# When two batches' loads begin in a fused sparse attention and feed-forward kernel

## The chip, the cores and the metric

The kernel runs on one core of a Trainium2 chip. The metric is the device time of one execution in microseconds (us). TensorE (PE) does the matmuls and PE transposes, VectorE (DVE) and ScalarE (ACT) the elementwise work, GpSimd (POOL) casts and copies and issues casting DMAs on its own queue, and SyncE (SP) issues the other DMAs, loads, stores and DMA transposes. All queues share 16 DMA engines.

## The reference

Eight batches, eight heads, 576 positions, head width 64. The first four heads attend to the last 32 positions, the other four to every 32nd position. The attention output, 4608 tokens by 512, goes through two matrices with a squared ReLU between them.

```python
scores = scale * np.matmul(q, k.transpose(0, 1, 3, 2))
mask_local = (rel >= 0) & (rel < stride)                  # heads 0-3
mask_strided = (rel >= 0) & (pos[None, :] % stride == pos[:, None] % stride)   # heads 4-7
attn = exp(masked scores - max); attn = attn / sum
x = np.matmul(attn, v).transpose(0, 2, 1, 3).reshape(B * S, H * D)
h = x @ w_in                 # 512 -> 2048
r = np.maximum(h, 0.0)
out = (r * r) @ w_out        # 2048 -> 512
```

All inputs and the output are float32; the kernel computes in bf16 with float32 accumulation.

## The kernel before

**Units.** Work on attention is cut into units of one batch and two heads: unit `u = 4 * b + p`. Of a batch's four units the first two are local, the other two strided. Batch 1 is units 4 to 7, batch 2 is units 8 to 11, and so on. A unit goes through `step_T` (PE transposes of q and k, line 271, read from the casts `q_l`, `k_l`; strided units from batch 2 on use DMA transposes instead), `step_S` (scores, line 315, then exp on ScalarE and the mask on VectorE), `step_D` (probabilities times V, line 419, and the division) and `step_E` (transposes back into `xt`, line 451).

**Feed-forward.** Tokens are cut into nine chunks of 512. `mm1` (line 487) is x times w_in, `mm2` (line 527) g times w_out. One `mm1` or `mm2` of four matmuls is a group, and the list `groups` is the backbone of the program. The attention steps of the next batches are threaded between the groups: `due[n]` says how many steps must have been emitted before group n. TensorE executes in exactly this order, so a step whose data is late stops everything behind it.

**Loads.** They hang on the same list: `plan` hooks `loads(b)` before a given group, and the queues then execute in the order written. Batch 2's hook is group 8, batch 3's is `g_end + 2`, group 33; the hook for batch 3's DMA transposes lies six groups behind it (`transpose_str`, line 161). A hook says only where a load stands in its queue's order. For batches 1 and 2 there is a data gate beside that: in `load_qk_local` GpSimd copies one element of another tile into the buffer that the first q load will overwrite (line 112), so that SP's load of q must wait for that copy, the copy for the transfer that fills the tile it reads, and everything behind either waits too. The gate of batch 1 reads the third quarter of w_in.

```python
if gate is not None and name == "q":
    nc.gpsimd.tensor_copy(t[0:1, 0, 0:1], gate)
```

**What stands behind the gate.** `loads(1)` issues on GpSimd, in this order: first quarter of w_out, q and k of unit 6, second quarter, local V of units 4 and 5, casts for unit 4, third quarter, q and k of unit 7, casts for unit 5, fourth quarter, then V of units 6 and 7 in two loads each (`load_v_str_cast`, line 227, into `vss[2]` and `vss[3]`), then two shifts. `loads(2)` and `loads(3)` put local q and k on SP as float32 (line 113), strided V on SP (line 201), cast strided q and k to DRAM by GpSimd's queue (line 153), load local V on GpSimd's queue (line 214), and then on GpSimd cast q and k (line 123, `q_st` to `q_l`, `k_st` to `k_l`), shift V (line 221) and cast strided V (line 208). The strided V tiles of a batch are `vss[0]` and `vss[1]` for even, `vss[2]` and `vss[3]` for odd batches. Buffers `q_st` and `k_st` are two deep, so a batch's q and k may be loaded once the batch before has been cast.

**Stores.** An output block is copied from PSUM to a tile `y` (four buffers) and stored by SP (line 532), in order with the loads.

Of the kernel before, what the change touches and what calls it, by code (L numbers as in the profile page):

```python
# [14 lines left out]
def kernel(  # L15
# [21 lines left out]
    NBS = 2 * NJ  # L37
# [28 lines left out]
    vss = [singles.tile([SP_, NBS, VP], BF16, name=f"vs{i}") for i in range(NV)]  # L66
# [4 lines left out]
    w_in_b = singles.tile([128, 4, d_ff], BF16)  # L71
    w_out_b = singles.tile([128, 16, d_model], BF16)
# [85 lines left out]
    def transpose_str(b):  # L158
        for name in "qk":
            o = strT.tile([128, NJ // 2, 4 * SP_], BF16, name=f"{name}T_s")  # L160
            nc.sync.dma_start_transpose(out=o, in_=big.pop((b, name)))
            for i in range(2):
                st.setdefault(4 * b + 2 + i, {})[name + "T"] = o[:, :, 2 * SP_ * i:2 * SP_ * (i + 1)]

    def transpose_local(u):
        s = st[u]
        for name in "qk":
            if name == "k":
                full = kTl[v_slot(u)]
                dst = full[:, 32:32 + S]  # L170
            else:
                full = dst = qkT.tile([128, S], BF16, name="qk"[u % 2] + "T")
            nc.sync.dma_start_transpose(out=dst.rearrange("c (t p) -> c t p", p=QL),
                                        in_=s[name].rearrange("p t h d -> p (t h d)"))
            s[name + "T"] = full
# [452 lines left out]

    pool2 = (nc.gpsimd.tensor_copy, nc.gpsimd.tensor_copy)

    gates = {1: w_in_b[0:1, 0, 1024:1025], 2: w_out_b[0:1, 8, 0:1]}

    def loads(b):
        u = 4 * b
        for i in range(2):
            load_qk_local(u + i, nc.sync, gate=gates.get(b) if i == 0 else None)
        if b == 1:
            load_w_out(0)
            load_qk_str(u + 2)
            load_w_out(1)  # L640
            for i in range(2):
                load_v_local_cast(u + i)
            cast_qk_local(u, pool2)
            load_w_out(2)
            load_qk_str(u + 3)
            cast_qk_local(u + 1, pool2)
            load_w_out(3)
            for i in range(2):
                load_v_str_cast(u + 2 + i)
            for i in range(2):  # L650
                shift_v_local(u + i)
            return
        load_v_str(u + 2, nc.sync)
        load_v_str(u + 3, nc.sync)
        cast_str_dram(b)
        for i in range(2):
            load_v_local_cast(u + i)
        for i in range(2):
            cast_qk_local(u + i, pool2)
        for i in range(2):  # L660
            shift_v_local(u + i)
        for i in range(2):
            cast_v_str(u + 2 + i)

    def loads_qk(b):
        for i in range(2):
            load_qk_local(4 * b + i, nc.sync)
        cast_str_dram(b)
        for i in range(2):
            cast_qk_local(4 * b + i, pool2)  # L670

    def loads_v(b):
        for i in range(2):
            load_v_local(4 * b + i, nc.sync)
        for i in range(2):
            load_v_str(4 * b + 2 + i, nc.sync)
        for i in range(2):
            cast_v_local(4 * b + i)
        for i in range(2):
            cast_v_str(4 * b + 2 + i)  # L680
# [89 lines left out]
    done_prev, g_prev = 0, 0  # L770
# [3 lines left out]
    def at(n, fn):  # L774
        hooks.setdefault(n, []).append(fn)

    def plan(b, n0, g0, g1):
        if b < LB:
            at(n0, lambda: loads(b))
            if b >= XB:  # L780
                at(n0 + 6, lambda: transpose_str(b))
            return
        g = g0 + (g1 - g0) * 45 // 100
        at(g, lambda: loads_qk(b))
        at(max(g + 8, g0 + (g1 - g0) * 8 // 10), lambda: transpose_str(b))
        at(n0, lambda: loads_v(b))
        for i in range(2):
            at(g + 14 + 4 * i, lambda u=4 * b + i: transpose_local(u))

    plan(2, 8, 0, 0)  # L790
    for b in range(1, B):
        g_end, s_end = ready.get(b, starts[b] - (14 if b >= XD else 2)), ends[4 * b + 3]
        if b == 1:
            g_prev = 12
        total = sum(weights[g_prev:g_end])
        for g in range(g_prev, g_end + 1):
            due[g] = done_prev + (s_end - done_prev) * sum(weights[g_prev:g]) // total
        if b + 2 < B:
            plan(b + 2, g_end + 2, g_prev, g_end)
        done_prev, g_prev = s_end, g_end  # L800
    done = 0
    for n, g in enumerate(groups):
# [40 lines left out]
```

## Time and profile before

| | before |
|---|---|
| five runs, us | 312.52, 314.27, 318.18, 324.10, 325.07 |
| median, us | 318.18 |
| profiled execution: its time, its span | 312.52, 310.6 us |
| mean granted TensorE clock | 0.995 |
| busy: TensorE, VectorE, ScalarE, GpSimd | 296.3, 166.6, 162.7, 88.2 us |
| DMA packets' time, SP's and GpSimd's queue | 50.1% and 26.2% of 16 engines' span |

The span runs from the first to the last instruction of one execution; its time includes what lies around that. The profiled execution is also the fastest of the five. The chain of work that ended last lists, in order of time, what each piece of the end's history waited for; the timeline lists instructions with the idle time before them in brackets and what ended it; a window gives each engine's busy time in a stretch, and the clock granted to TensorE there. A DMA's time to landing runs from its issue to the event that its data is there.

### The profile page before, as it was taken

How to read it: one execution, taken by the hardware profiler on the slowest of the kernel's cores; microseconds unless marked ns; L12 is line 12 of the kernel's file. 1: busy time of each engine (PE TensorE's matmuls, PEld its weight loads, DVE VectorE, ACT ScalarE, POOL GpSimd, SP SyncE). 2: the span in 40 equal slices, each digit the busy share in tenths (PEclk: the TensorE clock that was granted, in tenths of full speed). 3: DMA queues.
4: the chain of work that ended last, by engine and by line, in shares of the span. 5: the costliest groups of instructions: out<-in, count | busy, mean ns of one | idle time of the engine just before them, and what ended most of it. 6: DMA issues, size and time to landing. Idle time of an engine off the chain costs nothing.

```text
span 310.6 us, 6150 instructions
## 1 busy us (share of the span) xinstructions
PE 296.3 (95%) x2326; PEld 149.0 (48%) x2368; DVE 166.6 (54%) x411; ACT 162.7 (52%) x338; POOL 88.2 (28%) x117
## 2 busy tenths in 40 slices
PE   7889897999999999999999999999999999999995
PEld 3544454544555544454454454444444444444444
DVE  7675755479866966666468676654422222222200
ACT  3966654487555765555555555555343434344311
POOL 8528853654720712381065033000000000000000
PEclk9999999799999999999999999999999999999999
DMA  8999999999999999999999792224122000000121
GB/s 143 171 207 237 198 187 252 208 266 189 201 157 221 235 190 147 206 232 210 164 228 203 162 205 77 73 72 55 53 80 80 34 37 34 34 34 36 39 96 68
DMA packets 92252, 44.40 MB, mean 143 GB/s; under 512 B 76544, under 2 KB 85536, under 8 KB 92032
## 3 DMA queue, kind: packets, MB, share of 16 engines
q1 hardware_dynamic: 72528, 32.98, 50.1%
q0 software_dynamic: 19552, 10.98, 26.2%
q8 instruction: 18, 0.29, 0.4%
q10 hardware_dynamic: 144, 0.07, 0.1%
q14 instruction: 10, 0.08, 0.1%
HBM read 36.70 MB, written 13.57 MB: 162 GB/s over the span
## 4 chain that ended last, share of the span: by engine, by line
PE 80%; DMA 13%; POOL 4%; issue 1%; DVE 1%; ACT 0%; DVEq 0%; POOLq 0%; ACTq 0%
PE ph L487 36%; PE py L527 26%; PE ph L527 8%; DMA vs<-in_v_dram 5%; DMA w_in_b<-in_moe_w_in_dram 4%; PE pt L419 4%; DMA w_out_b<-in_moe_w_out_dram 4%; PE pt L315 3%; PE pt L451 1%; PE pt L271 1%; POOL kT_s L133 1%; POOL qT_s L133 1%; PE pt L512 1%; PE ph L512 1%; POOL vs L227 1%
## 5 line engine op out<-in xcount | busy, mean ns | idle before, releaser
L487 PE MATMUL ph<-xt,w_in_b 128*128 128x512 bf16 x559 | 142.2, 379 | 1.1 <-issue 0.3
L493 ACT ACTIVATE r<-ph 128x512 bf16<-128x512 f32 x143 | 85.3, 597 | 94.2 <-PE ph L487 91.3
L494 DVE TENSOR_TENSOR g_sb<-r 128x512 bf16<-128x512 bf16 x144 | 71.6, 502 | 101.9 <-ACT r L493 101.2
L527 PE MATMUL py<-w_out_b,g_sb 128*128 128x512 bf16 x378 | 99.6, 379 | 1.1 <-issue 0.3
L487 PEld LDWEIGHTS <-w_in_b 128*128 128x128 bf16 x576 | 52.4, 98 | 56.6 <-issue 0.5
L527 PEld LDWEIGHTS <-g_sb 128*128 128x128 bf16 x560 | 51.0, 98 | 53.8 <-issue 0.7
L320 ACT ACTIVATE e<-pt 128x288 bf16<-128x288 f32 (+1 forms) x128 | 46.3, 406 | 14.7 <-PE pt L315 14.7
L527 PE MATMUL ph<-w_out_b,g_sb 128*128 128x512 bf16 x155 | 39.3, 386 | 0.6 <-issue 0.3
L419 PEld LDWEIGHTS <-e 128*128 128x128 bf16 (+1 forms) x392 | 21.0, 98 | 17.3 <-issue 2.8
L434 DVE TENSOR_TENSOR x_s<-pt,rinv 72x384 bf16<-72x384 f32 (+1 forms) x42 | 21.4, 509 | 1.4
L192 POOL CAST vl<-vl_st 128x768 bf16<-128x768 f32 x8 | 6.6, 828 | 48.6 <-DMA vl_st<-in_v_dram 24.8
L326 DVE TENSOR_TENSOR e<-e,mask_str 72x576 bf16<-72x576 bf16 x32 | 17.1, 540 | 3.4 <-ACT e L320 3.2
L123 POOL CAST k_l<-k_st 96x768 bf16<-96x768 f32 x14 | 12.8, 913 | 17.0 <-DMA k_st<-in_k_dram 16.3
L531 ACT COPY y<-py 128x512 f32<-128x512 f32 x25 | 14.6, 585 | 5.5 <-PE py L527 5.1
L326 DVE TENSOR_TENSOR e<-e,mask_loc 128x576 bf16<-128x576 bf16 x32 | 15.6, 488 | 2.7 <-ACT e L320 2.7
L433 DVE RECIPROCAL rinv<-pt 96x6 f32<-96x6 f32 (+2 forms) x70 | 12.7, 182 | 7.5 <-PE pt L419 7.3
L123 POOL CAST q_l<-q_st 96x768 bf16<-96x768 f32 x14 | 12.5, 890 | 13.0 <-DMA q_st<-in_q_dram 11.1
L434 DVE TENSOR_TENSOR x_l<-pt,rinv 96x384 bf16<-96x384 f32 x28 | 15.5, 553 | 1.0
L419 PE MATMUL pt<-vs,e 72*128 72x65 bf16 x224 | 13.7, 196 | 2.3 <-DMA vs<-in_v_dram 2.2
L531 ACT COPY y<-ph 128x512 f32<-128x512 f32 x10 | 5.9, 587 | 16.0 <-PE ph L527 16.0
L208 POOL CAST vs<-v_st 72x1024 bf16<-72x1024 f32 x12 | 13.2, 1127 | 0.7 <-PE pt L451 0.4
L419 PE MATMUL pt<-vl,e 128*128 128x65 bf16 x168 | 9.8, 193 | 0.6 <-POOL vl L221 0.5
(91 smaller groups left out, 166.0 us busy)
## 6 DMA issues: line engine op xcount, KB each, us to landing
out_dram<-y SPq DMA_DIRECT2D x35, 256.0 KB, 2.9
v_st<-in_v_dram SPq DMA_DIRECT2D x12, 288.0 KB
q_st<-in_q_dram SPq DMA_DIRECT2D x16, 144.0 KB, 5.0
k_st<-in_k_dram SPq DMA_DIRECT2D x16, 144.0 KB, 7.0
vl_st<-in_v_dram SPq DMA_DIRECT2D x16, 144.0 KB, 3.0
w_in_b<-in_moe_w_in_dram POOLq DMA_DIRECT2D x4, 512.0 KB, 11.4
w_out_b<-in_moe_w_out_dram POOLq DMA_DIRECT2D x4, 512.0 KB, 10.4
q_st<-in_q_dram SPq DMA_DIRECT2D x7, 288.0 KB, 7.1
```

The source lines that it names most:

```text
L123: copy(t.rearrange("p j h d -> p h j d"), s[name + "f"].rearrange("p h (j d) -> p h j d", j=6))
L208: (copy or nc.gpsimd.tensor_copy)(t[:, :, 0:D], s["vf"].rearrange("p h (j d) -> p (h j) d", d=D))
L320: nc.scalar.activation(e[0:kn, lo:lo + S // 2], banks[row][half][0:kn, 0:S // 2], AF.Exp, scale=scale)
L326: nc.vector.tensor_tensor(x, x, m.to_broadcast([kn, n, w]), op=ALU.mult)
L419: nc.tensor.matmul(po[:, n - n0, :], e[0:kn, pos(n):pos(n) + 128], rhs[0:kn, src(n), 0:D + 1], start=True, stop=True)
L433: nc.vector.reciprocal(rinv[0:w, 0:m], po[0:w, 0:m, D:D + 1])
L434: nc.vector.tensor_tensor(x, po[0:w, 0:m, 0:D], rinv[0:w, 0:m].to_broadcast([w, m, D]), op=ALU.mult)
L487: nc.tensor.matmul(ph, w_in_b[:, kk, 128 * ff:128 * (ff + 1)], xt[kk][:, 512 * c:512 * (c + 1)], start=(kk == order[0]), stop=(kk == order ...
L493: nc.scalar.activation(r, ph, AF.Relu)
L494: later(1, lambda: nc.vector.tensor_tensor(g[:, ff, :], r, r, op=ALU.mult))
L527: nc.tensor.matmul(py, g[:, ff, 128 * j:128 * (j + 1)], w_out_b[:, ff, :], start=(ff == 0), stop=(ff == 15))
L531: nc.scalar.copy(y, py)
```

## The change

Two expressions. The gate of batch 2's loads reads an element of `vss[3]` that the last V load of batch 1 writes (its second half, `NBS - 1 = 15`), where it read the first element of the third quarter of w_out. And the hook of batch 3's loads is group 30 where it was 33, with its transposes at 36 where they were at 39; later batches keep their places.

```diff
-    gates = {1: w_in_b[0:1, 0, 1024:1025], 2: w_out_b[0:1, 8, 0:1]}
+    gates = {1: w_in_b[0:1, 0, 1024:1025], 2: vss[3][0:1, NBS - 1, 0:1]}
...
         if b + 2 < B:
-            plan(b + 2, g_end + 2, g_prev, g_end)
+            plan(b + 2, g_end + (2 if b > 1 else -1), g_prev, g_end)
```

In the emitted program TensorE's, VectorE's and ScalarE's instructions and their order are the same. On GpSimd the one copy reads another tile. On SP batch 3's six loads (four of q and k, two of V) stand ahead of the fourth output store instead of behind it.

## The prediction

> **What bounds the kernel now.** I read the page first: busy shares and the slices.
>
> ```profile
> PE 296.3 (95%) x2326; PEld 149.0 (48%) x2368; DVE 166.6 (54%) x411; ACT 162.7 (52%) x338; POOL 88.2 (28%) x117
> ...
> PE   7889897999999999999999999999999999999995
> ...
> PEclk9999999799999999999999999999999999999999
> DMA  8999999999999999999999792224122000000121
> ```
>
> TensorE is busy 95% of 310.6 us, so nothing later than the first 60 us has much to give. One slice (the eighth, 54 to 62 us) has a lower granted clock. Up to about 185 us the DMA engines are full: what a transfer gets, another loses. Next the chain of work that ended last, for the place where TensorE waits for a transfer; its longest single piece is (start, length, what):
>
> ```profile
> 38.68 15.29 DMA vs<-in_v_dram
> ```
>
> Then the timeline there, and the same microseconds as windows (PE busy, PEld, DVE, ACT, POOL, granted clock, DMA share, GB/s):
>
> ```profile
> 41.06 0.40 POOL L112 CAST q_st<-w_out_b 1x1 f32<-1x1 bf16 x1
> 41.49 0.31 SPq L113 DMA_DIRECT2D q_st<-in_q_dram  x1
> 50.51 0.82 POOL L123 CAST q_l<-q_st 96x768 bf16<-96x768 f32 x1 [3.14 <-DMA q_st<-in_q_dram]
> 54.01 0.31 PE L419 MATMUL pt<-vs,e 72*128 72x65 bf16 x5 [2.15 <-DMA vs<-in_v_dram]
> 57.53 0.69 PE L271 MATMUL pt<-ident,q_l 96*128 96x96 bf16 x6
> 59.46 0.42 PE L271 MATMUL pt<-ident,k_l 96*128 96x96 bf16 x6
> 63.03 0.42 PE L271 MATMUL pt<-ident,k_l 96*128 96x96 bf16 x6
> ```
>
> ```profile
> 55.00:56.00 1.00, 1.00 (x14) 0.79 (x12) 0.28 (x2) 0.26 (x1) 0.46 (x1) 0.64 0.80 169
> 56.00:57.00 1.00, 1.00 (x4) 0.30 (x2) 0.93 (x4) 0.00 (x0) 0.82 (x1) 0.50 1.61 153
> 57.00:58.00 1.00, 1.00 (x8) 0.62 (x7) 0.17 (x1) 0.00 (x0) 0.00 (x0) 0.50 2.34 149
> 58.00:59.00 1.00, 0.89 (x12) 0.74 (x12) 0.00 (x0) 0.69 (x2) 0.48 (x1) 0.65 0.72 31
> ```
>
> TensorE stands 2.15 us for unit 7's V (the last of batch 1), and then runs at half clock. Adding what is missing from 1.00 in the four windows, 0.36 + 0.50 + 0.50 + 0.35, gives 1.7 us. The stop so costs 3.8 us. The gate copy that today starts batch 2's loads ran at 41.06; batch 2's first cast (q of unit 8) waited for its data until 50.51, 9.0 us after issue, its k until 52.05. TensorE wanted them at 57.53 and 59.46: some 6 us of slack.
>
> **Part 1: the gate reads V instead of w_out.** No instruction is added; one 0.40 us copy on GpSimd waits for another transfer. The four V loads land, from the view of their tile and of single issues, 11.2, 10.9, 11.3 and 15.3 us after issue, that is at 46.6, 47.7, 49.2 and 54.0:
>
> ```profile
> L227 POOL DMA_DIRECT2D vs<-in_v_dram x4: 804/809/828, 35.4 to 38.7; - x4
> ...
> DMA to landing us min/median/max: 10.9/11.3/15.3
> ```
>
> The first three are 1.1 and 1.5 us apart, the last is 4.8 behind, just when SP's queue starts to move batch 2 (its first packets show between 45 and 46 us). Taking that traffic away, the last V lands early at 48.0 (most of the V packets, all under 512 B, had moved by 46; two us for the end), late at 54.0 (the tail is its own queue's). I take 49.5: near 38.68 + 10.9. TensorE wants V at 51.9, so the 2.15 us and the 1.7 us of slow clock go: -3.8 us, with 2.4 us of cover.
>
> The pause and the clock have a rule too. The Trainium skill (TensorE: Matmul & The Clock Gate, Part 1: The HAM clock gate) says that the clock halves after about 3.4 us idle; here 2.15 us were followed by 0.50 from 55 to 58.6 us. By the rule alone a pause this short need not cost clock, and the gain would be 2.15 us; the measured row decides.
>
> **What the later gate queues up.** On GpSimd behind the copy: two casting DMAs of q and k to DRAM, two loads of local V, four casts, two shifts, two V casts, and all of batch 3. On SP behind its wait for that copy: batch 2's q, k and strided V loads, two transposes, the output stores, batch 3's loads. All move from 41.5 to 49.9 us, 8.4 later, against a TensorE that comes 3.8 us sooner. Without the stop it would want q of unit 8 at 54.4, k at 55.7, unit 9's q at 56.8 and k at 59.2.
>
> How fast do they land in an emptier queue? Two other batches say:
>
> ```profile
> 22.93 0.31 SPq L113 DMA_DIRECT2D q_st<-in_q_dram  x1
> 27.65 0.85 POOL L123 CAST q_l<-q_st 96x768 bf16<-96x768 f32 x1
> 29.82 0.98 POOL L123 CAST k_l<-k_st 96x768 bf16<-96x768 f32 x1 [1.33 <-DMA k_st<-in_k_dram]
> ...
> 61.67 0.49 SPq L113 DMA_DIRECT2D q_st<-in_q_dram  x1
> 65.37 0.98 POOL L123 CAST q_l<-q_st 96x768 bf16<-96x768 f32 x1 [0.33 <-DMA q_st<-in_q_dram]
> 70.55 1.11 POOL L123 CAST k_l<-k_st 96x768 bf16<-96x768 f32 x1 [4.21 <-DMA k_st<-in_k_dram]
> ```
>
> Batch 1 had its first k 6.9 us after the first issue, batch 3 8.9; q came after at most 4.7 and 3.7. Batch 2 itself took 9.0 and 10.6, but behind the V loads. I take 4.2 for q and 7.9 for k, between the two emptier cases. Then q of unit 8 lands at 54.1, its cast (0.85) ends at 54.9: 0.5 us late. k lands at 57.8, cast until 58.7, wanted at 56.2: 2.5 late. Unit 9's q (about 9.5 after issue, then 0.85) is there at 60.2, wanted at 59.8: 0.4 late; its k (11.4 in batch 3) at 62.2, wanted 62.6: in time. So 3.4 us of the 3.8 come back, as the same kind of stop one transfer later. Bounds: nothing comes back but 0.5 (gate at 48.0, batch 1's pace: k cast by 56.2), or all and more (next part, third rival). Whether the new 2.5 us pause also costs clock, as the 2.15 did, would add up to 1.7; several short pauses with work between I cost at 0.
>
> The rule against waiting: the Trainium skill (DMA: Bandwidth & Descriptors, Anatomy of one DMA) puts about 2.0 us of fixed time on each DMA, which a load that starts only after another has landed pays in series. By its formula 288 KB would take 2.7 us (an estimate), q would be ready by 53.4 and its 0.5 us of lateness gone; no row here shows one so quick.
>
> Further behind: local V for unit 8 is issued at about 51 and lands 11.7 (batch 1) to 13.3 (batch 3) later, 62.7 to 64.3, then a 0.7 us shift; wanted at 67.2 less 0.4: covered by about 2 us, 0 if TensorE keeps the whole gain. The transposes for unit 10 were issued by 59.5 and used at 70.26; about 4 us later they are still covered.
>
> **Part 2: batch 3 three groups sooner.** Nothing is added; one 256 KB store of SP's goes behind six loads, and two transposes are queued sooner. On GpSimd batch 3's DMAs (62.25) already followed batch 2's last cast (60.28, 2.02 long) without a gap, so the sooner place brings nothing there; on SP at most one store's issue, 0.5 us. With batch 2's tail some 4 us later, batch 3 is later, not sooner; its tightest use is k of unit 12, cast until 71.7 and wanted at 78.98: 7.3 us of cover. The delayed store holds a y buffer not needed before 81.47. Cost 0; if that cover is gone, a stop of the size it is short.
>
> **Sum.** -3.8 + 3.4 = -0.4 us on the profiled 312.52 us (span 310.6): 312.1. That execution is the fastest of five (312.52 to 325.07); the median lies 5.7 above. Only this transfer-paced stage shows where a slower run can lose time: V has no reserve before, 2.4 us after. I let a third of the 5.7 remain, 1.9: 314.0. That third is a choice, between none and all (312 to 318).
>
> **The rivals.**
> - *Full gain* (0.25). Gate at 48.0, batch 1's pace: only 0.5 comes back, 309.2; with at most 1 us of the runs' offset, 310. For it: V's packets were nearly all through by 46. Against: DMA engines stand idle while the gate's landing is awaited (46 to 50 us moved 0.9 MB before).
> - *Batch 2 late* (0.22), the slower side. If the loads need as long after the gate as they do now (9.0, 10.6, about 13.1 and 14.4) with V at 50.3 and the copy done at 50.7: q of unit 8 cast by 60.6, wanted 54.4, 6.2 us; k 0.2 more; unit 9's q at 64.6, wanted 63.2, 1.4 more. -3.8 + 7.8 + 1.7 of clock = +5.7, 318.2; with the whole offset of 5.7, 324. It decides from k of unit 8 cast after 59.5 on: 55.7 + 3.8. For it: four casting loads share the engines. Against: V is no longer in front of them.
> - *V no sooner* (0.08). The change does not do what it says: V at 54.0, no gain, gate copy done at 54.4, q 2.0, k 1.8 and unit 9's q 0.4 late: +4.2, 316.7, with the offset 322.
> - *Forecast* (0.45): the stop moves from V to k. Own range 310 to 319.
>
> **How the numbers follow.** A difference of about 2% (311.8, 324.5) is what a measurement of this kernel can tell. Faster: 0.12 of the forecast and 0.23 of full gain, 0.35. Slower: 0.02 of the forecast, 0.20 of late batch 2, 0.05 of the late V, 0.27. Within: 0.38. Range: from the full gain with no offset, rounded to 308.5, to the late batch 2, 324.5.
>
> **What would show it.** Right: no wait of line 419 for vs near 52 us; gate copy at 48 to 51; waits of line 271 for q_l or k_l of 1 to 4 us between 54 and 62; batch 3 some 4 us later on GpSimd, harmless. Wrong: V still at 54 (step of part 1), k in time (the pace), a wait at line 315 for the transposes or at line 419 for vl (cover behind), or stops after 75 us (part 2).

## The result, and the profile after

| | before | changed |
|---|---|---|
| median of all runs, us (lowest to highest; number) | 312.80 (309.70 to 325.07; 80) | 314.44 (312.17 to 316.73; 43) |
| changed / before | | 1.0074 [1.0059, 1.0090] |
| profiled execution: its time, its span | 312.52, 310.6 us | 315.88, 314.0 us |
| mean granted clock | 0.995 | 0.989 |

The changed kernel is 0.7% slower. That is small, and the forecast's sign was wrong. A repeat of the same kernel in a later comparison (g0_changed) gave 1.0029 [0.9996, 1.0063]; between the two the loss is some 0.3 to 0.7%. The ratios leave disturbed executions out on both sides and the medians don't, and where only a disturbed execution was profiled (f3, g2, h4, i2) its profile isn't used.

The spread moved too, and the other way: 12 of the 80 runs of before took more than 317 us, none of the 43 of the changed kernel did. Over all runs the means are 313.79 and 314.36, only 0.2% apart. What follows is about the ratio; why before's long runs are missing behind the later gate isn't shown here.

The page of the changed kernel, its busy shares and 40 slices:

```profile
span 314.0 us, 6149 instructions
...
PE 298.5 (95%) x2326; PEld 149.1 (47%) x2368; DVE 169.6 (54%) x411; ACT 162.5 (52%) x338; POOL 89.8 (29%) x117
...
PE   7879989699999999999999999999999999999995
PEclk9999999789999999999999999999999999999999
DMA  7999996999998998999899887224122100000021
```

The shape is that of before: the dip of PE and of its clock is still in the eighth slice, the clock now over two slices. Only what stands in the dip has changed. The chain of work that ended last (start, length, what), two of its pieces:

```profile
39.26 9.38 DMA vs<-in_v_dram
49.33 8.81 DMA k_st<-in_k_dram
```

Unit 7's V takes 9.38 us where it took 15.29, and unit 8's k has joined the chain right behind it. The timeline shows the same instructions that the prediction followed:

```profile
48.76 0.18 POOL L112 CAST q_st<-vs 1x1 f32<-1x1 bf16 x1 [7.28 <-DMA vs<-in_v_dram]
48.96 0.31 SPq L113 DMA_DIRECT2D q_st<-in_q_dram  x1
52.52 0.82 POOL L123 CAST q_l<-q_st 96x768 bf16<-96x768 f32 x1 [0.34 <-DMA q_st<-in_q_dram]
52.14 0.35 PE L419 MATMUL pt<-vs,e 72*128 72x65 bf16 x6
58.26 0.82 POOL L123 CAST k_l<-k_st 96x768 bf16<-96x768 f32 x1 [4.92 <-DMA k_st<-in_k_dram]
59.14 0.66 PE L271 MATMUL pt<-ident,k_l 96*128 96x96 bf16 x6 [2.82 <-POOL k_l L123]
65.65 0.42 PE L271 MATMUL pt<-ident,k_l 96*128 96x96 bf16 x6
```

The gate copy runs at 48.76 (41.06 before). TensorE goes through V at 52.14 without a stop, then waits 2.82 us for unit 8's k (unit 8's q, cast by 53.34, was in time). From there to unit 9's k it takes 65.65 - 59.14 = 6.51 us; before it was 63.03 - 59.46 = 3.57. The windows (PE busy, PEld, DVE, ACT, POOL, granted clock, DMA share, GB/s) say why:

```profile
60.00:62.00 2.00, 2.00 (x11) 1.09 (x10) 0.60 (x1) 0.45 (x1) 1.01 (x2) 0.50 1.90 105
62.00:64.00 2.00, 2.00 (x14) 0.68 (x14) 0.42 (x1) 0.99 (x3) 0.69 (x1) 0.50 0.97 101
64.00:66.00 2.00, 2.00 (x19) 0.96 (x14) 0.43 (x1) 0.78 (x3) 0.02 (x1) 0.66 1.42 99
```

TensorE is never idle there, at half clock. So in this execution the stop moved from V to k and took the slow clock with it: 6.51 - 3.57 = 2.9 us. Unit 9's k is 2.6 us later than before and the end 3.4.

That is one execution. What the profiles with the V gate have in common lies further back, in a relay of steps that each wait for the one before or stand in a queue behind it: GpSimd casts batch 3's strided q and k to DRAM (line 153), SP transposes them (line 161), then loads batch 4's local q and k (line 107) and, once they are cast, transposes those (line 173; k goes into `kTl`). In the timelines of GpSimd and SP, before and then changed:

```profile
62.25 0.52 POOL L153 DMA_DIRECT2D q_d<-in_q_dram  x1
67.84 3.71 SPq L161 DMA_TRANSPOSE qT_s<-q_d  x1
76.47 1.45 SPq L107 DMA_DIRECT2D q_st<-in_q_dram  x2
103.13 1.69 SPq L173 DMA_TRANSPOSE kTl<-k_l  x1
```

```profile
69.35 0.52 POOL L153 DMA_DIRECT2D q_d<-in_q_dram  x1
76.97 1.37 SPq L161 DMA_TRANSPOSE qT_s<-q_d  x1
82.54 1.08 SPq L107 DMA_DIRECT2D q_st<-in_q_dram  x2
108.04 1.23 SPq L173 DMA_TRANSPOSE kTl<-k_l  x1
```

Batch 3's strided casts to DRAM (line 153) come 7.1 us later, the transposes of SP that read them 9.1, batch 4's loads behind these on SP 6.1, and the last DMA transpose for unit 17, in batch 4, 4.9. SP has few gaps for catching up: in before the lengths of its issues from 76.47 to 103.13 add up to 25.3 of 26.7 us. Not all of that need be work: the view of SP's waits puts some 9 us of this stretch down to waiting for other engines, 4.5 of them for VectorE. In the repeat g0_changed TensorE was not stopped at unit 8 and was ahead, with unit 9's k at 60.59 against 63.03. TensorE's timeline of before at unit 17's scores, and then of that run:

```profile
109.53 0.43 PE L315 MATMUL pt<-kT,kTl 64*128 64x96 bf16 x12
```

```profile
60.59 0.42 PE L271 MATMUL pt<-ident,k_l 96*128 96x96 bf16 x6
...
74.22 0.33 PE L315 MATMUL pt<-qT_s,kT_s 64*72 64x72 bf16 x7 [0.86 <-DVE x_l L434]
100.10 0.43 PE L315 MATMUL pt<-qT,kTl 64*128 64x96 bf16 x12 [1.46 <-DMA kTl<-k_l]
110.41 0.43 PE L315 MATMUL pt<-kT,kTl 64*128 64x96 bf16 x12 [1.25 <-DMA kTl<-k_l]
```

It stops for the transposes of units 16 and 17, 50 us behind the change. Unit 17's scores, the last of these lines, start at 110.41 against 109.53 before: from 2.4 us ahead to 0.9 behind.

The start of unit 17's scores is a good mark: in the ten profiles of this table the span ends 201.1 us behind it, but for e2 (201.7) and e4 (202.1). Times of the relay, us:

| kernel | gate copy of batch 2 | line 153, batch 3 | first line 107, batch 4 | unit 17's last transpose issued | unit 17's scores | span |
|---|---|---|---|---|---|---|
| before | 41.06 | 62.25 | 76.47 | 103.13 | 109.53 | 310.6 |
| e2_hook (old gate) | 42.33 | 65.72 | 78.79 | 104.04 | 108.08 | 309.8 |
| f2_before_hoist (old gate) | 41.73 | 56.55 | 77.13 | 104.75 | 108.71 | 309.8 |
| g1_gate_w4 (w_out's fourth quarter) | 45.64 | 66.15 | 78.64 | 104.56 | 108.63 | 309.7 |
| changed | 48.76 | 69.35 | 82.54 | 108.04 | 112.95 | 314.0 |
| g0_changed | 48.71 | 68.11 | 81.65 | 105.69 | 110.41 | 311.5 |
| e1_gate | 49.02 | 68.94 | 82.03 | 106.92 | 111.33 | 312.4 |
| e3_fill_k | 47.38 | 67.55 | 80.59 | 105.79 | 110.95 | 312.0 |
| e4_unit8_early | 42.20, then 50.83 | 65.69 | 80.23 | 107.30 | 111.19 | 313.3 |
| f4_before_late (old gate) | 41.55 | 75.84 | 85.22 | 108.86 | 113.32 | 314.4 |

f4, in which batch 3 is held back by hand, aside: in this table, with a gate on w_out the mark lies at 108.1 to 109.5, with the V gate (e4's second) at 110.4 to 113.0. The groups don't overlap. Their means, 108.7 and 111.4, lie 2.6 us apart, somewhat more than the loss in the times (0.3 to 0.7% of 312.8 is 0.9 to 2.3).

Last, the transfers, in windows of before and then of the changed kernel:

```profile
45.00:50.00 5.00, 4.91 (x68) 2.98 (x69) 2.96 (x8) 2.75 (x8) 0.89 (x1) 1.00 1.33 215
```

```profile
45.00:50.00 5.00, 4.94 (x67) 2.86 (x66) 3.06 (x9) 2.69 (x7) 0.93 (x3) 1.00 0.93 52
```

215 against 52 GB/s: while the gate waits for V's landing, little else may move. Summed over windows from 40 us, before has moved 1.99 MB by 50 us and 14.74 by 110, the changed kernel 1.23 and 13.94: some 0.8 MB are missing at both. But the second isn't simply the first carried on. g0_changed is 0.70 MB short at 50 us and 0.35 at 110; e4, whose gate lets unit 8 pass, 0.14 and then 0.59; f4, with the old gate and no gap, nothing at 50 and 0.88 at 110.

### The profile page after: what moved, and what is told of

Same layout as the page of the kernel before. It is cut to its first block, busy times and chain, and to the rows that moved or that the text cites. A ratio compares the mean times of both kernels' runs of the same rounds, so it can differ in the third digit from the quotient of the medians.

```text
span 314.0 us, 6149 instructions
## 1 busy us (share of the span) xinstructions
PE 298.5 (95%) x2326; PEld 149.1 (47%) x2368; DVE 169.6 (54%) x411; ACT 162.5 (52%) x338; POOL 89.8 (29%) x117
## 4 chain that ended last, share of the span: by engine, by line
PE 76%; DMA 13%; POOL 4%; DVE 3%; issue 2%; ACT 0%; SPq 0%; POOLq 0%; DVEq 0%; ACTq 0%
PE ph L487 33%; PE py L527 26%; PE ph L527 8%; DMA w_in_b<-in_moe_w_in_dram 4%; DMA w_out_b<-in_moe_w_out_dram 3%; PE pt L419 3%; DMA vs<-in_v_dram 3%; PE pt L315 3%; DMA k_st<-in_k_dram 3%; DVE g_sb L494 2%; PE pt L451 1%; PE pt L271 1%; POOL kT_s L133 1%; POOL qT_s L133 1%; DVE e L326 1%
## 5 line engine op out<-in xcount | busy, mean ns | idle before, releaser
L487 PE MATMUL ph<-xt,w_in_b 128*128 128x512 bf16 x559 | 144.5, 384 | 1.1 <-issue 0.3
L494 DVE TENSOR_TENSOR g_sb<-r 128x512 bf16<-128x512 bf16 x144 | 73.7, 516 | 102.1 <-ACT r L493 101.7
L527 PE MATMUL ph<-w_out_b,g_sb 128*128 128x512 bf16 x155 | 38.4, 379 | 0.5 <-issue 0.3
L192 POOL CAST vl<-vl_st 128x768 bf16<-128x768 f32 x8 | 7.6, 950 | 50.9 <-PE pt L315 25.8
L326 DVE TENSOR_TENSOR e<-e,mask_loc 128x576 bf16<-128x576 bf16 x32 | 17.9, 558 | 3.4 <-ACT e L320 3.4
L326 DVE TENSOR_TENSOR e<-e,mask_str 72x576 bf16<-72x576 bf16 x32 | 16.0, 505 | 3.4 <-ACT e L320 3.3
L123 POOL CAST k_l<-k_st 96x768 bf16<-96x768 f32 x14 | 12.1, 866 | 10.2 <-DMA k_st<-in_k_dram 10.0
L208 POOL CAST vs<-v_st 72x1024 bf16<-72x1024 f32 x12 | 13.9, 1184 | 0.4
```

The costliest lines, as they stand in the source:

```text
L123: copy(t.rearrange("p j h d -> p h j d"), s[name + "f"].rearrange("p h (j d) -> p h j d", j=6))
L208: (copy or nc.gpsimd.tensor_copy)(t[:, :, 0:D], s["vf"].rearrange("p h (j d) -> p (h j) d", d=D))
L326: nc.vector.tensor_tensor(x, x, m.to_broadcast([kn, n, w]), op=ALU.mult)
L487: nc.tensor.matmul(ph, w_in_b[:, kk, 128 * ff:128 * (ff + 1)], xt[kk][:, 512 * c:512 * (c + 1)], start=(kk == order[0]), stop=(kk == order ...
L494: later(1, lambda: nc.vector.tensor_tensor(g[:, ff, :], r, r, op=ALU.mult))
L527: nc.tensor.matmul(py, g[:, ff, 128 * j:128 * (j + 1)], w_out_b[:, ff, :], start=(ff == 0), stop=(ff == 15))
```

## Experiments

**Which half of the change?** e1_gate takes the gate alone, e2_hook the hook alone.

```diff
e1  gates = {..., 2: vss[3][0:1, NBS - 1, 0:1]}     (hook g_end + 2 as before)
e2  plan(b + 2, g_end + (2 if b > 1 else -1), ...)  (gate w_out_b as before)
```

> The gate alone, batch 3's place as before. Theory A (the gate makes the whole difference: the stop moves from V of unit 7 to k of unit 8, and the clock is paid again): as the changed kernel, about 314.4 us, a wait of TensorE at line 271 for k_l of 2 to 4 us near 57 us, V by 49. Theory B (batch 3's sooner place costs the time): within 0.5 us of before, 312.8.

> Batch 3's sooner place alone, the gate as before. Theory A: as before, 312.8 us within 0.5, the wait for V of unit 7 still there, batch 3's first load less than 1 us sooner. Theory B: 1 to 2 us slower than before.

e1: 1.0021 [0.9988, 1.0053]. e2: 0.9992 [0.9956, 1.0029]. The hook does nothing that can be told, as predicted; the gate alone isn't told from before by its time either. Its interval lies below the 1.0059 to 1.0090 of the whole change's first comparison and takes in g0's 1.0029, so the times don't say how the loss divides. The gate's profile has the late stops all the same, and nearly no early one:

```profile
57.72 0.43 PE L271 MATMUL pt<-ident,k_l 96*128 96x96 bf16 x6 [0.36 <-POOL k_l L123]
...
100.98 0.43 PE L315 MATMUL pt<-qT,kTl 64*128 64x96 bf16 x12 [1.50 <-DMA kTl<-k_l]
111.33 0.43 PE L315 MATMUL pt<-kT,kTl 64*128 64x96 bf16 x12 [1.29 <-DMA kTl<-k_l]
```

**Is it the clock, or unit 8's lateness?** e3_fill_k is the changed kernel with 13 matmuls into an unused PSUM tile ahead of unit 8's k. In e4_unit8_early unit 8's q and k go at the old gate, and the V gate holds only what follows.

```diff
e3  fill(13); step_T(8, "k")
e4  gate=(gates.get(b) if i == 0 else gate9 if b == 2 else None)   # gates[2]: w_out_b, gate9: vss[3]
```

> The changed kernel with 13 idle matmuls of 128x512 (2.8 us at full clock, their result unused) right ahead of the transposes of unit 8's k. Theory A, the clock part: the idle matmuls lie in the wait for k, the granted clock stays at 1.00 and the 3.5 us at half clock go: 1.5 to 2 us faster than the changed kernel, about 312.6. Rival (the wait itself and VectorE's later jam are the loss, the clock is not): no gain, up to 1 us slower where k comes early.

> The changed kernel, but unit 8's q and k (0.6 MB) keep the old gate, the third quarter of w_out; only unit 9's q and k and all behind them wait for V. Theory A (late k of unit 8 is the loss): V of unit 7 at 48 to 51, unit 8's k cast by 56, no wait at line 271 over 1 us, no clock loss; 309.5 to 311 us. Rival (the loads share the engines so that V is then as late as before): a wait for V of 1 to 2 us returns and the time is that of before, 312 to 313.

e3: 1.0066 [1.0035, 1.0097]. TensorE's timeline and one window:

```profile
55.52 2.97 PE L550 MATMUL py<-w_in_b 128*128 128x512 bf16 x13
58.33 0.42 PE L271 MATMUL pt<-ident,k_l 96*128 96x96 bf16 x6
```

```profile
59.00:61.00 2.00, 2.00 (x25) 1.02 (x23) 0.97 (x2) 1.35 (x3) 0.07 (x1) 1.00 1.37 89
```

The clock held at 1.00 and the time is still 0.7% above. Since the matmuls themselves take TensorE 3.0 us, which cost time where k comes early, e3 alone doesn't settle it; the clocks on record do. In 21 of the changed kernel's 44 executions on record the mean granted clock was 0.998 or more, and their median is 314.44, that of all; 34 of before in the experiments' comparisons had as much, with a median of 312.00. The slow clock is real in the changed kernel's profiled execution, but it isn't the loss. e4: 1.0047 [1.0011, 1.0082], with no stop at unit 8 and stops of 1.49 and 1.29 us for `kTl`. So a loss remains where unit 8 is in time, and the lateness of all behind it is what is left.

**Batch 3's place.** f1 (on the changed kernel), f2 (on before) and f3 (on e4) issue batch 3's casting DMAs of line 153 right after batch 2's casts. f4 does the reverse to before: it puts them behind batch 3's four casts.

```diff
     load_v_str(...)
-    cast_str_dram(b)
+    if b != 3: cast_str_dram(b)
     ... cast_qk_local of both units
+    if b == 2: cast_str_dram(3)      # f1, f2, f3
+    if b == 3: cast_str_dram(3)      # f4
```

> The changed kernel, with batch 3's two casting DMAs of q and k to DRAM moved on GpSimd's queue from behind batch 2's shifts and V casts to right behind its q and k casts. Theory C (the late gate is paid downstream: GpSimd's tail delays batch 3's casting DMAs, these SP's transposes and so batch 4's loads and transposes, for which line 315 waits near 100 and 110 us): the casting DMAs go out near 61 us instead of 69, SP's transposes for batch 3 start near 70 instead of 77, batch 4's last transpose is issued 4 us or more sooner, no wait at line 315 near 110, and 1.5 to 2.5 us faster than the changed kernel: 312 to 313. Theory A (the loss is the wait for k of unit 8 and its clock): as the changed kernel, 314 to 314.5.

> The kernel before with the same move. Theory C: the gain is small, 0 to 1 us, since in the kernel before batch 4's transposes are just in time or at most 0.6 us late. A gain of 2 us or more would say that the kernel before already pays there.

> Unit 8's q and k at the old gate, the rest of batch 2 at V's, and the same move. Both the early stops and the late ones should go. Theory C: no wait above 1 us for V, for k of unit 8 or for batch 4's transposes; 309.5 to 311 us, faster than both kernels. Theory A: as the run with unit 8 early alone, 314 to 315.

> The kernel before, gate and hooks untouched, but batch 3's two casting DMAs put behind batch 3's four casts on GpSimd: issued near 74 us instead of 62. Theory C: SP's transposes for batch 3 start near 80 instead of 68, batch 4's last transpose is issued 6 to 10 us later, line 315 waits 3 us or more near 100 to 112, and the kernel is 3 to 6 us slower than before. Theory A: batch 2 is untouched, so at most 1 us slower.

f1: 1.0106 [1.0063, 1.0150], f2: 1.0007 [0.9965, 1.0050], f3: 1.0115 [1.0045, 1.0185], f4: 1.0107 [1.0059, 1.0155]. f4 shows what batch 3's lateness alone costs, with the old gate: line 153 at 75.84 against 62.25, and 1.1% of the time. (Its profiled execution also stopped 3.10 us for V, so that its 113.32 for unit 17 isn't the relay's alone.) The cure did not work: in f1 line 153 came at 60.41, but another transfer paid:

```profile
70.57 0.47 PE L315 MATMUL pt<-qT_s,kT_s 64*72 64x72 bf16 x16 [2.12 <-DMA kT_s<-k_d]
```

Batch 2's own transposes were now late, and those of units 16 and 17 as before (1.21, 1.89). What goes ahead takes the place of something else. In f2, with the old gate, the same hoist changed nothing.

**A gate in between, and what batch 4 is worth.** g0 is the changed kernel again. g1 gates on the fourth quarter of w_out, landing between the third and V. g3 is the changed kernel without batch 4's four DMA transposes (units 16 and 17 then use old contents).

```diff
g1  gates = {..., 2: w_out_b[0:1, 12, 0:1]}
g3  def transpose_local(u):  if u in (16, 17): ...; return
```

> The changed kernel itself, so that the next runs can be compared with it on the same chip: 0.6 to 0.9% slower than before in every theory. Theory C expects that its profile shows a late stop (line 315 near 100 or 110 us) where the early stop for k of unit 8 is short, and none where it is long.

> The kernel before with batch 2's gate on the fourth quarter of w_out, which lands 4 to 5 us after the third and 2 to 8 before V. Theory C (each us of delay goes down the relay of GpSimd and SP): between before and the changed gate, 0 to 0.3% slower, V in time or up to 1 us late, SP's transposes of batch 3 about 3 us later than before. Theory D (what counts is V's stop, and it goes when V is relieved): up to 0.5% faster, since V is in time and k of unit 8 too.

> The changed kernel without the four DMA transposes of batch 4's local q and k (units 16 and 17 take stale tiles instead). Theory C (the relay's end at line 315 for units 16 and 17 sets the time): no wait there, 1 to 3 us faster than the changed kernel on the same chip. Theory A (k of unit 8 and the clock set it): the same as the changed kernel within 0.7 us.

g1: 1.0020 [0.9982, 1.0058], its copy at 45.64. No stop for V, waits of 1.19 and 0.65 us for `kTl`, and unit 17 at 108.63: by the ratio as good as before, no better. Its 12 runs lie between 310.35 and 314.53, though, where the 35 of before beside them reach 324.26. g3: 0.9984 [0.9958, 1.0010], 0.45% below g0 in the same comparison: without those four transposes the loss is gone. Since they took queue time and bytes too, and before without them wasn't run, that supports the relay and doesn't prove it.

**What was V's stop worth?** g2 leaves out unit 7's V loads (it uses unit 6's V), so that unit 7 has none of its own to wait for, and two loads of 72 KB are gone; unit 6's, then the last to be issued, can still be late. h4 keeps the old gate and puts ten matmuls ahead of the stop, so the clock has less cause to drop.

```diff
g2  load_v_str_cast(u + 2) only;  st[u + 3]["v"] = vss[2]
h4  fill(10); step_D(7, 0)
```

> The kernel before without the two loads of unit 7's V; unit 7 multiplies by unit 6's V instead. So TensorE can't wait for that V, and batch 2 starts as early as before or sooner. The prediction took the stop and its clock as 3.8 us, which this would gain: 309. Theory C: batch 4's transposes are ready only 1 to 1.5 us before TensorE comes today, so a TensorE 3 us sooner waits at line 315 near 108: gain 0.5 to 2 us, 311 to 312.5.

> The kernel before with 10 idle matmuls of 128x512 (2.2 us, result unused) ahead of unit 7's first multiplication by V, to hold the clock where V is late. The prediction counts 1.7 us of clock in the stop, so up to 1.7 us faster. Theory C: what comes sooner waits again at unit 17, so within 0.7 us of before; and where V is in time the idle matmuls cost up to 2.2 us, of which the same slack hides 1 to 1.5.

g2: 0.9929 [0.9889, 0.9969]; h4: 0.9990 [0.9947, 1.0033]. 0.7% of 312.8 is 2.2 us (by the interval 1.0 to 3.5), and that with two loads less; the 3.8 of the sum (1.2%) lie just outside. h4 shows no gain from the clock, but its interval reaches 1.7 us of gain, and where V is in time its matmuls cost some. The executions themselves say more: of the 107 of before that the experiments' ratios keep, the 34 with a granted clock of 0.998 or more have a mean of 312.0 us, the other 73 one of 312.9. The other profiles agree that the term is too large: of five with the old gate in place, V's stop is 2.15 (before), 2.57 (f2), 3.10 (f4), 0.15 (h2) and none (e2). It isn't in every execution. And f2 with its stop,

```profile
54.80 0.31 PE L419 MATMUL pt<-vs,e 72*128 72x65 bf16 x5 [2.57 <-DMA vs<-in_v_dram]
```

reaches unit 17 at 108.71, e2 without one at 108.08. Two us won at 54 are mostly gone again before 110 (e2 waits 0.54 us there, f2 0.32).

**SP's order.** If the relay were only a matter of SP's queue, moving batch 4's four local transposes ahead of its strided ones, the stores and the V loads should undo it: h1 on the changed kernel, h2 on before, h3 on g1.

```diff
+    if b == 4: transpose_local(16) and (17) ahead of transpose_str(4)
```

> The changed kernel with nothing left out: on SP's queue batch 4's four transposes of local q and k go ahead of its two strided transposes, two stores and six V loads, where units 16 and 17 had been behind them. Theory C: the stops at line 315 near 100 and 110 us go, 1 to 2 us faster than the changed kernel, 312 to 312.7, level with before or just under. Theory A (the early stop is the loss): as the changed kernel.

> The kernel before with the same order on SP. Theory C: gain 0 to 1.5 us, since those of its executions in which V is in time are held at unit 17 (0.3 to 0.6 us in two profiles); none in those in which V is late.

> The gate on w_out's fourth quarter with the same order on SP: V in time, k of unit 8 in time, and no late stop. Theory C: 310 to 311.5 us, faster than before by 0.4 to 0.9%. If the transposes' place does not matter: as with that gate alone, 312.5.

h1: 1.0077 [1.0044, 1.0109], h2: 1.0111 [1.0068, 1.0155], h3: 1.0030 [0.9998, 1.0062]. Unit 17 does come sooner (108.54, 107.42, 106.38), and the gain is lost behind it. TensorE in h2:

```profile
145.73 1.39 PE L487 MATMUL ph<-xt,w_in_b 128*128 128x512 bf16 x3 [2.56 <-DMA xt<-x_l]
```

There is the same wait of 0.86 us in h1 and 1.33 in h3. It is only part of what is lost: from unit 17's scores to the end h1 takes 203.5, h2 205.6 and h3 204.1 us, where 201.1 is usual. The order of SP alone isn't the cause either; here too another transfer became the last.

**Fewer bytes.** i1 (changed) and i2 (before) cut the first eight stores to 128 columns: the same instructions, 1.5 MB less, the rest of 1024 rows isn't written.

```diff
+            w = 128 if c < 2 else 512
-            nc.sync.dma_start(out=out[r0:r0 + 128, :], in_=y)
+            nc.sync.dma_start(out=out[r0:r0 + 128, 0:w], in_=y[:, 0:w])
```

> The changed kernel with the first eight stores of output blocks cut from 512 to 128 columns (the rest of these 1024 rows is left out): 1.5 MB less to move before 110 us, every instruction and every order kept. Theory E (the transfers are the shared limit up to some 180 us, and the gate wastes 4 us of them): the stops at line 315 near 100 and 110 us shrink by more than half and it is 1 to 2 us faster than the changed kernel: level with before. Theory F (SP's and GpSimd's order and issue times alone): within 0.5 us of the changed kernel.

> The same cut in the kernel before. Theory E: it has the 0.4 to 0.8 MB in hand, so it gains less than the changed kernel, 0 to 1 us. If both gain alike, the smaller stores tell nothing about the gate.

i1: 1.0008 [0.9973, 1.0042], i2: 0.9977 [0.9945, 1.0010]. In i1's profile the waits for `kTl` are gone (unit 17 at 109.01, span 310.1) and the longest stop behind 60 us is

```profile
75.47 0.33 PE L315 MATMUL pt<-qT_s,kT_s 64*72 64x72 bf16 x7 [1.73 <-DVE x_l L434]
```

But the distance between i1 and i2, 0.3%, is that between changed and before within the intervals. That fewer bytes cure the late stops was seen in one profile; that they cure the loss was not shown.

## Why the prediction was wrong, point by point

- **V lands sooner, its stop goes: right.** Gate at 48.76 (49.5 predicted), no wait of line 419 for `vs`.
- **k of unit 8 late by 2.5, q by 0.5, unit 9's q by 0.4: right for k in the profiled execution, not for the two q.** k landed 8.81 us after its issue (7.9 taken), TensorE waited 2.82; for neither q did it wait. Unit 8's q landed 3.6 us after its issue, between the 4.2 taken and the 2.7 that the prediction worked out from the Trainium skill (DMA: Bandwidth & Descriptors, Anatomy of one DMA), whose formula is fitted on DMAs that GpSimd issues, while this load is SP's. In other executions TensorE waited 0.36 us for k (e1) or not at all (g0), so k in time, the condition of the full gain, did occur, and with it the end still came 0.9 us later (g0).
- **Size of the gain, 3.8 us: too large.** It was read from one execution in which V's stop and its slow clock were both present. Over executions it is some 2.2 us (g2, 1.0 to 3.5 by its interval). The term lacked the question how often the stop occurs, and five runs between 312.52 and 325.07 couldn't answer it.
- **Clock of the new pause, "cost at 0": wrong in the profiled execution**, 2.9 us against a named bound of 1.7. The executions without it (median 314.44) show that it isn't what makes the kernel slower on the whole. The Trainium skill (TensorE: Matmul & The Clock Gate, Part 1: The HAM clock gate) speaks of about 3.4 us without work and of a window that runs free of the program. The runs fit the second and not the first as a threshold: half clock came with pauses of 2.15 us (before), 2.82 (changed) and 3.10 (f4), and none with the 2.57 of f2.
- **"Batch 3 is later, not sooner ... 7.3 us of cover ... Cost 0": the step that failed.** Batch 3's lateness was right (line 153 7.1 us later) and so was its cover: no wait for unit 12's k followed. But the step asked only what batch 3 needs, and stopped there. Batch 3's transposes hold SP for batch 4's loads, and those for the transposes of units 16 and 17 at 100 and 110 us, which have no cover: in before the last is issued 6.4 us ahead of unit 17's scores, and in g0, where TensorE waits, 4.7. So the changed gate gives back what it wins, even where unit 8's k is in time (g0: 3.3 us more than before from unit 9's k to unit 17's scores). Where the sum has 0 for this step and -0.4 us in all, the changed kernel lost 0.9 to 2.3 us (0.3 to 0.7% of 312.8). "Stops after 75 us" stood among the signs of error; no rival had it as its mechanism: the full gain met its condition in g0 without the gain, the late batch 2 needed k cast after 59.5 (it was cast by 59.08), and V was not late. "Nothing later than the first 60 us has much to give" had asked only what could be won there, not what could be lost.
- **The offset.** The five runs' median of 318.18 was a poor draw: 80 runs give 312.80, the profiled 312.52 was an ordinary execution, and between the profiled execution and the median there was no offset of 5.7 us to divide. Of the 4.2 us by which the forecast lay under that median, 3.8 were this offset and 0.4 the sum's. So 314.0 lies near 314.44 by luck, by two errors that cancel: a loss left out and an offset put in. What held is that the spread is narrower, 312.17 to 316.73, with none over 317 us where before has 12 of 80; that this is V's reserve wasn't shown.

**What stays open.** The stops at batch 4's transposes come with the V gate (e1, whose time alone shows no loss) and with what follows unit 8 (e4); g0 and e3 have them too, and lateness of batch 3 alone makes a loss like it (f4). Whether the transposes are late because bytes missed in the gap must still be moved, or because SP's queue has few gaps and keeps its order, the runs don't separate: SP's order alone doesn't cure it (h1), fewer bytes did so in one profile (i1), and both act on the same queue.

The page DMA: Bandwidth & Descriptors of the Trainium skill (Rules for kernel authors) advises to issue a transfer early and to wait for it late. A gate does the reverse to every load behind it; here the ratios of later gates were level (g1) or slower, and none was faster.

## What to carry to other kernels

When a whole stream of loads is moved, don't stop at the first consumer: follow each queue until the delay meets an idle stretch, and where a queue has few gaps (25.3 of 26.7 us taken) expect it to arrive at whatever has least cover, here 50 us on. Before pricing a stop from one profile, ask in how many executions it occurs, and take no median of five widely spread runs for the baseline. Look at the spread beside the ratio: here the gate costs 0.3 to 0.7% by the ratio and the runs over 317 us are gone.

## What was not expected of the hardware

- A pause of 2.57 us (f2) left the clock at 1.00 in every window from 50 to 76 us, one of 2.15 (before) did not.
- DMA transposes stand long on SP's queue: one of batch 3's from DRAM 1.3 to 4.9 us in the profiles of the table and f1's, a local one of batch 4's 1.2 to 2.1. How much of that is waiting isn't shown.
- V's four loads of 72 KB took 9.4 to 11.8 us each in the changed kernel, though between 45 and 50 us only 52 GB/s were moving; the last, issued at 39.26, needed 9.38.
